# Decode scratch in PSUM, ELU with one VectorE pass, and a moved accumulator, in an LSH attention + Mish MoE + ELU MoE kernel on one core

## The chip, the cores and the metric

One core of a Trainium2 chip runs the whole program. The metric is the device time of one execution in microseconds (us), lower is better. Engines are named as in the profile: PE (TensorE matmul), PEld (its weight load), DVE (VectorE), ACT (ScalarE), POOL (GpSimd), SP (the engine that issues most transfers).

## The reference

Three layers follow each other; each one's output is the next one's x. Shapes: 2 batches, 8 heads, 768 tokens, head width 64; 1536 tokens in all, model width 512, inner width 2048.

```python
# 1. attention; a query sees the keys that hash into its bucket (6 sign bits)
mask   = q_bucket[:, :, :, None] == k_bucket[:, :, None, :]
scores = np.where(mask, scale * q @ k.T, -1e9)
x = softmax(scores) @ v                          # -> (1536, 512)
# 2. feed-forward with Mish
h = x @ w_in                                     # (1536, 2048)
x = (h * np.tanh(softplus(h))) @ w_out
# 3. feed-forward with ELU
h = x @ w_in2
y = np.where(h > 0, h, np.exp(np.minimum(h, 0)) - 1) @ w_out2
```

The weights arrive in HBM as 64-bit floats, and are turned into 32-bit parts on the chip.

## The kernel before

**Arithmetic.** TensorE multiplies in fp32r. To keep the precision each operand is split in a high and a low part, and a product is three matmuls: high*high, high*low, low*high (`products`, line 681). A 128x512 output needs 4 blocks of the inner dimension, so 12 matmuls. The split of an activation is an ACT cast (high) and a subtraction (low), `split`, line 753.

**Order.** No loop order is written down. Each operation is recorded with its engine, a cost, what it comes after and a priority, and a list scheduler (`Plan.run`, line 133) sets the order on every engine; buffers are rings (`Ring`), and an operation that needs a new buffer also waits for the last user of the oldest one. The planner's costs set the order alone; the chip then runs each engine's list in that order, each instruction waiting on semaphores. Attention with the first three weight units is planned first, the two feed-forward layers after it.

**Feed-forward.** The weights are 64 units of 128x512 numbers, 32 for each layer, half of them w_in and half w_out. An "up" step makes one accumulator h{unit}_{chunk} (a PSUM bank) from x and a unit, applies Mish or ELU and splits it into g{unit}_{chunk}; a "down" step sums four g into y_acc. There are three chunks of 512 tokens. Within the Mish layer, from unit 6 on, pairs of units do their chunks 0 and 2 in seven half products in place of eight (`pair_step`, line 758; banks b1 to b4, temporaries p and q from the ring gg_r); the sums of x that they need (T0, T1, T2) are made once by `turn` (line 833), which uses y_acc as scratch before y_acc is needed. `turn` runs 8 additions x_hi + x_lo, 8 subtractions, 8 ACT casts and 8 low parts; its additions and subtractions may go to DVE or POOL.

**Weight decode** (`convert`, line 271). A unit's raw 64-bit words (wraw) become a float by five DVE passes: L294 (shift and mask), L297 (and/or), L300 (compare and multiply), L302 (mask), L305 (low word times scale), one ACT Square (L292), then one ACT cast and two POOL passes make the high and low part w. Its scratch t, s (`wt`, `ws`) is in SBUF, two buffers of each.

**PSUM.** Eight banks. In the feed-forward layers six are the ring h_r, two the ring e_r: it holds the chunk-1 accumulators of the Mish layer, and in the ELU layer the exponentials.

**ELU** (`elu`, line 741). ACT makes exp(h) into e_ and tanh(h/2) into gg, DVE makes gg = (e_ + 1) * gg, which is exp(h) - 1, and then max(min(gg, 0), h).

**Reuse of SBUF.** When attention ends, the pool mp lies over attention's pool from the same address. A tile's first use waits for the last users of the attention tiles under it. y_acc is mp's first tile (24 KB per partition); the first tiles of attention's pool are ident, cst, sp (2.2 KB together; ident is the identity that every transpose reads, the last ones being those of rb, L590), then the heads' buffers.

Of the kernel before, what the change touches and what calls it, by code (L numbers as in the profile page):

```python
# [199 lines left out]
def kernel(ctx, tc, qk, v, w, tab, out):  # L200
# [70 lines left out]
    def convert(p, u, prio, keep=False):  # L271

        raw, ld = RAW.pop(u)
        t, s, w_ = Buf(wt_r, f"wt{u}"), Buf(ws_r, f"ws{u}"), Buf(wu_r, f"w{u}")

# [18 lines left out]
        o2 = p.op({DVE: dve(n, True)}, lambda e: nc.vector.tensor_scalar(  # L294
            out=ti(), in0=high(), scalar1=3, scalar2=0x3FFFFFF8, op0=ALU.logical_shift_left, op1=ALU.bitwise_and),
            [ld], [raw, t], prio, port=True)
        o3 = p.op({DVE: dve(n)}, lambda e: nc.vector.scalar_tensor_tensor(  # L297
            out=ti(), in0=high(), scalar=-0x40000000, in1=ti(), op0=ALU.bitwise_and, op1=ALU.bitwise_or),
            [o2], [raw, t], prio, port=True)
        o4 = p.op({DVE: dve(n)}, lambda e: nc.vector.scalar_tensor_tensor(  # L300
            out=t.tile, in0=s.tile, scalar=2.0 ** -30, in1=t.tile, op0=ALU.is_ge, op1=ALU.mult), [o1, o3], [s, t], prio, port=True)
        o5 = p.op({DVE: dve(n, True)}, lambda e: nc.vector.tensor_scalar(  # L302
            out=s.tile.bitcast(I32), in0=ti(), scalar1=-0x800000, scalar2=None, op0=ALU.bitwise_and),
            [o4], [s, t], prio, port=True)
# [19 lines left out]
    def sums(p, ue, uo, prio):  # L324
# [751 lines left out]
```

## Time and profile before

| | |
|---|---|
| median of 3 runs | 760.56 us (760.34 to 765.42) |
| profiled execution | 760.42 us, its span 758.6 us |
| PE busy | 744.9 us, 98% |
| DVE busy | 643.0 us, 85% |
| ACT, POOL busy | 431.0 us (57%), 363.1 us (48%) |
| chain that ended last | PE 78%, DVE 16%, ACT 2%, POOL 1% |

The span runs from the first to the last instruction; 1.8 us of the execution lie around it. PE's busy time alone doesn't tell what can be gained, since the ends of pipelined matmuls are modelled: the number of matmuls in a stretch and the distance from start to start do.

### The profile page before, as it was taken

The numbers are of one execution on the slowest core, as the hardware profiler recorded it, in microseconds if no ns is written. First come the engines' busy times: TensorE is split into PE (matmuls) and PEld (weight loads), VectorE is DVE, ScalarE is ACT, GpSimd is POOL, SyncE is SP. The second block draws the span as 40 slices with busy tenths as digits, with TensorE's granted clock in tenths as the row PEclk, the third lists the DMA queues.
The fourth block names the chain that finished last, engine by engine and source line by source line (L and its number), as shares of the span: only waits on it lengthen the run. The fifth ranks groups of instructions, "written<-read, shape, count | busy, mean of one in ns | idle before, by whom it ended". The sixth has DMA issues, their size and how long they took to land.

```text
span 758.6 us, 11117 instructions
## 1 busy us (share of the span) xinstructions
PE 744.9 (98%) x3936; PEld 645.8 (85%) x3936; DVE 643.0 (85%) x1118; ACT 431.0 (57%) x845; POOL 363.1 (48%) x274
## 2 busy tenths in 40 slices
PE   8999999999999799999999999999999999999998
PEld 7999999999988678888888888887888888888886
DVE  7899998999988989577696779999999999999442
ACT  5788888888885545543443346356556544443310
POOL 4345834743565655646536465863444423434100
PEclk9999999999999899999999999999999999999999
DMA  7776777686510121122111311112222212120012
GB/s 206 196 196 177 173 183 181 159 206 157 142 50 1 56 84 56 58 87 78 56 56 55 112 56 56 59 57 81 83 84 84 84 56 84 56 83 29 1 69 98
DMA packets 26983, 72.89 MB, mean 96 GB/s; under 512 B 6048, under 2 KB 7216, under 8 KB 26928
## 3 DMA queue, kind: packets, MB, share of 16 engines
q1 hardware_dynamic: 26784, 72.17, 32.3%
q8 instruction: 31, 0.51, 0.3%
q14 instruction: 24, 0.20, 0.1%
q10 hardware_dynamic: 144, 0.01, 0.0%
HBM read 45.76 MB, written 3.19 MB: 65 GB/s over the span
## 4 chain that ended last, share of the span: by engine, by line
PE 78%; DVE 16%; ACT 2%; issue 2%; POOL 1%; DMA 0%; DVEq 0%; POOLq 0%; ACTq 0%
PE h L688 47%; PE xt L575 8%; PE st L503 8%; PE tu L562 7%; PE h_b L688 7%; DVE ws L305 2%; DVE wt L297 2%; PE pj L425 2%; DVE wt L294 2%; DVE wt L300 2%; DVE ptl L258 1%; DVE g L258 1%; DVE pt L506 1%; DVE ws L302 1%; DVE gg L747 1%
## 5 line engine op out<-in xcount | busy, mean ns | idle before, releaser
L688 PE MATMUL h<-g,w 128*128 128x512 f32 x1140 | 267.0, 390 | 2.3 <-DVE g L258 1.6
L688 PEld LDWEIGHTS h<-g,w 128*128 128x128 f32 x1140 | 213.7, 188 | 48.5 <-DVE g L258 2.7
L688 PE MATMUL h<-x_hi,w 128*128 128x512 f32 x576 | 187.3, 394 | 3.9 <-DVE g L258 3.9
L258 POOL TENSOR_TENSOR wt<-wt,w 128x512 f32<-128x512 f32 x52 | 76.1, 1465 | 178.5 <-ACT w L253 84.9
L688 PEld LDWEIGHTS h<-x_hi,w 128*128 128x128 f32 x576 | 109.4, 190 | 27.1 <-DVE g L258 4.3
L688 PE MATMUL h<-x_lo,w 128*128 128x512 f32 x288 | 113.0, 392 | 0.0
L258 DVE TENSOR_TENSOR ptl<-tu,pth 128x512 fp32r<-128x512 f32 x144 | 96.1, 686 | 12.9 <-ACT pth L567 11.9
L511 ACT ACTIVATE pt<-pt,nb 128x768 f32<-128x768 f32 x96 | 90.4, 944 | 8.4 <-DVE nb L509 8.0
L567 ACT CAST pth<-tu 128x512 fp32r<-128x512 f32 x144 | 79.8, 587 | 26.4 <-PE tu L562 25.8
L506 DVE TENSOR_SCALAR_CACHE_REDUCE pt<-st 128x768 f32<-128x768 f32 x96 | 89.1, 950 | 1.4 <-PE st L503 0.9
L503 PE MATMUL st<-qkt 76*128 76x384 f32 (+1 forms) x384 | 81.5, 344 | 1.5 <-DVE qkt L432 0.8
L253 ACT CAST w<-wt 128x512 fp32r<-128x512 f32 x64 | 39.7, 623 | 73.0 <-DVE wt L300 50.6
L317 POOL TENSOR_TENSOR w<-wt,ws 128x512 fp32r<-128x512 f32 x52 | 72.5, 1394 | 17.5 <-DVE ws L305 12.8
L562 PE MATMUL tu<-ident,pt 128*128 128x128 f32 x576 | 80.0, 274 | 0.7 <-DVE ptl L258 0.6
L575 PE MATMUL xt<-pth,vt 128*128 128x256 f32 x288 | 79.1, 304 | 0.0
L983 DVE TENSOR_TENSOR y_acc<-h,y_acc 128x512 f32<-128x512 f32 x71 | 47.8, 686 | 32.5 <-PE h L688 32.4
L575 PE MATMUL xt<-ptl,vt 128*128 128x256 f32 x288 | 72.9, 282 | 0.0
L562 PEld LDWEIGHTS tu<-ident,pt 128*128 128x128 f32 x576 | 66.7, 140 | 5.9 <-DVE ptl L258 1.8
L503 PEld LDWEIGHTS st<-qkt 76*128 76x128 f32 (+1 forms) x384 | 64.1, 189 | 2.8 <-DVE pt L506 1.5
L253 ACT CAST g<-h 128x512 fp32r<-128x512 f32 x72 | 42.3, 587 | 40.6 <-DVE h L749 40.1
L305 DVE SCALAR_TENSOR_TENSOR ws<-wraw,ws 128x512 f32<-128x512 uint32 x64 | 64.0, 1000 | 0.9
L294 DVE TENSOR_SCALAR wt<-wraw 128x512 int32<-128x512 int32 x64 | 47.4, 746 | 20.3 <-POOL w L258 19.4
(106 smaller groups left out, 1149.1 us busy)
## 6 DMA issues: line engine op xcount, KB each, us to landing
wraw<-in_w_dram SPq DMA_DIRECT2D x64, 512.0 KB
qkt<-z SPq DMA_DIRECT2D x30, 384.0 KB
rw<-in_qk_dram SPq DMA_DIRECT2D x16, 384.0 KB
qkt<-z SPq DMA_DIRECT2D x31, 192.0 KB
vr<-in_v_dram SPq DMA_DIRECT2D x8, 384.0 KB
out_dram<-y_acc SPq DMA_DIRECT2D x11, 256.0 KB
rr<-dr SPq DMA_DIRECT2D x14, 192.0 KB
xs<-xr SPq DMA_DIRECT2D x14, 192.0 KB
```

Of the source, the lines that this page charges most:

```text
L253: nc.scalar.copy(out=out, in_=in_)
L258: eng(e).tensor_tensor(out=out, in0=a, in1=b, op=ALU.subtract)
L294: o2 = p.op({DVE: dve(n, True)}, lambda e: nc.vector.tensor_scalar(out=ti(), in0=high(), scalar1=3, scalar2=0x3FFFFFF8, op0=ALU.logical_sh ...
L305: o6 = p.op({DVE: dve(n)}, lambda e: nc.vector.scalar_tensor_tensor(out=s.tile, in0=low().bitcast(U32), scalar=2.0 ** -52, in1=s.tile, op0 ...
L317: o9 = p.op({POOL: pool(n)}, lambda e: nc.gpsimd.tensor_tensor(out=lo(), in0=t.tile, in1=s.tile, op=ALU.add), [o6, o8], [t, s, w_], prio)
L503: nc.tensor.matmul(st.tile[:, c, 0:HS], lhsT=wt.tile[0:n, q, t * 128:(t + 1) * 128], rhs=wt.tile[0:n, 2 + q, c * HS:(c + 1) * HS], start=( ...
L506: o = max_op = p.op({DVE: dve(S)}, lambda e: nc.vector.tensor_scalar(out=half(pt.tile), in0=st.tile[:, :, 0:HS], scalar1=-MASKED / SCALE, ...
L511: o = p.op({ACT: act(S, False) + 196}, lambda e: nc.scalar.activation(out=pt.tile, in_=pt.tile, func=AF.Exp, bias=nb.tile, scale=SCALE, ac ...
L562: nc.tensor.transpose(tu.tile[:, k, j], pt.tile[:, (2 * b + k) * 128:(2 * b + k + 1) * 128], ident)
L567: o = p.op({ACT: act(512)}, lambda e, tu=tu, ks=ks: nc.scalar.copy(out=hi.tile[:, ks], in_=flat(tu)), [o], [tu, hi], order(i, 'hi'))
L575: nc.tensor.matmul(xt.tile[:, 0:TH], lhsT=vt.tile[:, k, g % 2], rhs=m.tile[:, k], start=(k == 0 and j == 0), stop=(k == NKT - 1 and j == 1))
L688: nc.tensor.matmul(t.tile, lhsT=w_.tile[:, a, k], rhs=r, start=(start and n == 0), stop=(stop and n == 3 * len(ks) - 1), skip_group_check= ...
```

## The change

Four edits, taken together.

1. **Decode.** From unit 3 on (c_r is given), three scratch tiles a, b, d of a unit come from c_r, a ring over the two PSUM banks that were e_r: b is L294's result, a is Square's, d is L302's. The float t, the low part s and the parts w stay in SBUF. Every DVE pass of the decode then has a PSUM operand, and the planner no longer treats it as sharing a port with POOL; L294 is recorded ahead of Square.
2. **Accumulators.** Chunk-1 accumulators of the Mish layer go to h_r, which has the other six banks.
3. **ELU.** ACT makes Relu(-h) into gg, then exp(-gg) in place, DVE makes max(gg - 1, h): two ACT passes as before, one after the other, and one DVE pass in place of two.
4. **Layout.** gg_r has four buffers, and they are allocated first in mp (the "gap" tiles), so y_acc starts 8 KB further in, past ident, cst and sp. The scratch that the compiler reserves for dynamic DMA is 2 KB in place of 16, which makes room. The additions of `turn` go to POOL alone, and POOL passes are planned with other costs (pool2).

The core of the diff (renamed arguments of the other decode passes are left out; line numbers move by 6 to 12):

```diff
...
-    def convert(p, u, prio, keep=False):
+    def convert(p, u, prio, keep=False, c_r=None):
...
+        a, b, d = (Buf(c_r, f"c{u}_{i}") for i in range(3)) if c_r else (s, t, s)
+        port = not c_r
...
+        o2 = p.op({DVE: dve(n, port)}, lambda e: nc.vector.tensor_scalar(
+            out=bits(b), in0=high(), scalar1=3, scalar2=0x3FFFFFF8, op0=ALU.logical_shift_left, op1=ALU.bitwise_and),
+            [ld, *(HELD if c_r else ())], [raw, t, b], prio, port=port)
         o1 = p.op({ACT: act(n, False)}, lambda e: nc.scalar.activation(
-            out=s.tile, in_=high().bitcast(F32), func=AF.Square), [ld, *HELD], [raw, s], prio)
...
+            out=a.tile, in_=high().bitcast(F32), func=AF.Square), [ld, *HELD, o2 if c_r else None], [raw, s, a], prio)
...
-            out=s.tile, in0=low().bitcast(U32), scalar=2.0 ** -52, in1=s.tile, op0=ALU.mult, op1=ALU.mult),
-            [o5], [raw, s], prio, port=True)
+            out=s.tile, in0=low().bitcast(U32), scalar=2.0 ** -52, in1=d.tile, op0=ALU.mult, op1=ALU.mult),
+            [o5], [raw, s, d], prio, port=port)
+        cost = pool2(n) if c_r else pool(n)
...
-        y_acc = mp.tile([128, NX, NT], F32, name="y_acc")
...
-        gg_r = ring(3, [128, TC], F32, "gg")
+        gg_r = ring(NGG, [128, TC], F32, "gg")
+        [mp.tile([128, TC], F32, tag="gg", name=f"gap{i}", bufs=NGG) for i in range(NGG)]
+        y_acc = mp.tile([128, NX, NT], F32, name="y_acc")
...
-        e_r = Ring(2, lambda n: banks[1].tile([128, TC], F32, tag="e", name=n, bufs=2))
+        c_r = Ring(2, lambda n: banks[1].tile([128, TC], F32, tag="e", name=n, bufs=2))
...
             a = p.op({ACT: act(n)}, lambda e: nc.scalar.activation(
-                out=e_.tile, in_=t.tile, func=AF.Exp), [x, table[0]], [t, e_], prio)
-            b = p.op({ACT: act(n)}, lambda e: nc.scalar.activation(
-                out=gg.tile, in_=t.tile, func=AF.Tanh, scale=0.5), [x, table[0]], [t, gg], prio)
+                out=gg.tile, in_=t.tile, func=AF.Relu, scale=-1.0), [x, table[0]], [t, gg], prio, lat=60)
+            a = p.op({ACT: act(n, False)}, lambda e: nc.scalar.activation(
+                out=gg.tile, in_=gg.tile, func=AF.Exp, scale=-1.0), [a, table[0]], [gg], prio)
             a = p.op({DVE: dve(n)}, lambda e: nc.vector.scalar_tensor_tensor(
-                out=gg.tile, in0=e_.tile, scalar=1.0, in1=gg.tile, op0=ALU.add, op1=ALU.mult), [a, b], [e_, gg], prio)
-            a = p.op({DVE: dve(n)}, lambda e: nc.vector.scalar_tensor_tensor(
-                out=t.tile, in0=gg.tile, scalar=0.0, in1=t.tile, op0=ALU.min, op1=ALU.max), [a], [t, gg], prio)
+                out=t.tile, in0=gg.tile, scalar=1.0, in1=t.tile, op0=ALU.subtract, op1=ALU.max), [a], [t, gg], prio)
...
-                    t = Buf(e_r if kind == 0 and c == 1 else h_r, f"h{u}_{c}")
+                    t = Buf(h_r, f"h{u}_{c}")
...
```

**What moves on the engines.** PE's list is the same up to the first pair of units, and holds the same matmuls to the end. DVE's list is the same to the end of attention, and is then another one. Its first twelve entries after the last low part of x, before (g is an activation's low part, wt, ws decode scratch, wraw a raw unit; the number behind a name's last underscore only tells buffers apart):

```order
L294 TENSOR_SCALAR wt3_3692<-wraw3_3159 128x512
L294 TENSOR_SCALAR wt4_3696<-wraw4_3351 128x512
L297 SCALAR_TENSOR_TENSOR wt3_3692<-wraw3_3159,wt3_3692 128x512
L258 TENSOR_TENSOR g0_0_3694<-h0_0_3465,g0_0_3694 128x512
L258 TENSOR_TENSOR g1_0_3714<-h1_0_3605,g1_0_3714 128x512
L300 SCALAR_TENSOR_TENSOR wt3_3692<-ws3_3690,wt3_3692 128x512
L297 SCALAR_TENSOR_TENSOR wt4_3696<-wraw4_3351,wt4_3696 128x512
L302 TENSOR_SCALAR ws3_3690<-wt3_3692 128x512
L300 SCALAR_TENSOR_TENSOR wt4_3696<-ws4_3710,wt4_3696 128x512
L305 SCALAR_TENSOR_TENSOR ws3_3690<-wraw3_3159,ws3_3690 128x512
L302 TENSOR_SCALAR ws4_3710<-wt4_3696 128x512
L258 TENSOR_TENSOR g2_0_3730<-h2_0_3612,g2_0_3730 128x512
```

And the same place of the changed kernel, on DVE too (c is the scratch in PSUM):

```order
L303 TENSOR_SCALAR c3_1_3695<-wraw3_3159 128x512
L303 TENSOR_SCALAR c4_1_3701<-wraw4_3351 128x512
L264 TENSOR_TENSOR g0_0_3698<-h0_0_3465,g0_0_3698 128x512
L308 SCALAR_TENSOR_TENSOR wt3_3694<-wraw3_3159,c3_1_3695 128x512
L308 SCALAR_TENSOR_TENSOR wt4_3700<-wraw4_3351,c4_1_3701 128x512
L264 TENSOR_TENSOR g1_0_3718<-h1_0_3605,g1_0_3718 128x512
L311 SCALAR_TENSOR_TENSOR wt3_3694<-c3_0_3725,wt3_3694 128x512
L311 SCALAR_TENSOR_TENSOR wt4_3700<-c4_0_3739,wt4_3700 128x512
L313 TENSOR_SCALAR c3_2_3747<-wt3_3694 128x512
L313 TENSOR_SCALAR c4_2_3754<-wt4_3700 128x512
L316 SCALAR_TENSOR_TENSOR ws3_3724<-wraw3_3159,c3_2_3747 128x512
L316 SCALAR_TENSOR_TENSOR ws4_3738<-wraw4_3351,c4_2_3754 128x512
```

The decode of units 3 and 4 now runs side by side, and g0_0 stands one place earlier. Further on in DVE's list of before, the entries that lead up to g3_0, the low part that the down step of unit 4 waits for:

```order
L258 TENSOR_TENSOR g2_1_3856<-h2_1_3797,g2_1_3856 128x512
L258 TENSOR_TENSOR g2_2_3863<-h2_2_3816,g2_2_3863 128x512
L302 TENSOR_SCALAR ws5_3827<-wt5_3829 128x512
L258 TENSOR_TENSOR T1_1_3678<-y_acc_3674,T1_1_3678 128x512
L305 SCALAR_TENSOR_TENSOR ws5_3827<-wraw5_3760,ws5_3827 128x512
L258 TENSOR_TENSOR T2_1_3680<-y_acc_3674,T2_1_3680 128x512
L294 TENSOR_SCALAR wt6_3904<-wraw6_3784 128x512
L258 TENSOR_TENSOR g3_0_3902<-h3_0_3844,g3_0_3902 128x512
```

The same place on DVE in the changed kernel:

```order
L264 TENSOR_TENSOR g2_1_3873<-h2_1_3809,g2_1_3873 128x512
L316 SCALAR_TENSOR_TENSOR ws5_3847<-wraw5_3774,c5_2_3875 128x512
L264 TENSOR_TENSOR g2_2_3882<-h2_2_3833,g2_2_3882 128x512
L264 TENSOR_TENSOR T1_1_3682<-y_acc_3678,T1_1_3682 128x512
L264 TENSOR_TENSOR T2_1_3684<-y_acc_3678,T2_1_3684 128x512
L311 SCALAR_TENSOR_TENSOR wt6_3827<-c6_0_3900,wt6_3827 128x512
L313 TENSOR_SCALAR c6_2_3923<-wt6_3827 128x512
L316 SCALAR_TENSOR_TENSOR ws6_3899<-wraw6_3781,c6_2_3923 128x512
L264 TENSOR_TENSOR g3_0_3925<-h3_0_3861,g3_0_3925 128x512
```

The whole decode of unit 6 now stands ahead of g3_0, where one pass of it stood before. From the last low part of x up to g3_0 DVE has 36 entries before and 37 now. On POOL the passes of `turn` still stand right behind the last entry of attention.

## Rows read from the trace of the kernel before

**Rows 1.** The page: busy time of each engine (share of the span) and instructions.

```profile
PE 744.9 (98%) x3936; PEld 645.8 (85%) x3936; DVE 643.0 (85%) x1118; ACT 431.0 (57%) x845; POOL 363.1 (48%) x274
```

**Rows 2.** Windows: stretch, length, busy PE, PEld, DVE, ACT, POOL; granted clock; DMA.

```profile
235.00:262.00 27.00, 23.13 (x92) 18.63 (x91) 25.69 (x28) 14.36 (x26) 21.06 (x14) 0.87 0.12 40
...
300.00:500.00 200.00, 200.00 (x881) 165.03 (x880) 157.40 (x227) 88.96 (x158) 116.88 (x92) 1.00 0.19 66
500.00:540.00 40.00, 38.70 (x170) 31.50 (x169) 39.28 (x63) 25.84 (x49) 15.84 (x12) 1.00 0.19 66
```

**Rows 3.** PE's longest waits after 240: line, releaser, us in total, times, longest.

```profile
PE h L688 <- DVE g L258: 5.4, 4, 3.9
```

**Rows 4.** Timeline of PE, 247 to 261: start, us, operation, count [idle before].

```profile
248.52 0.39 PE L688 MATMUL h<-x_hi,w 128*128 128x512 f32 x1
252.78 0.79 PE L688 MATMUL h<-x_hi,w 128*128 128x512 f32 x1 [3.87 <-DVE g L258]
...
258.66 0.62 PE L688 MATMUL h<-x_hi,w 128*128 128x512 f32 x2
```

**Rows 5.** Timeline of DVE, 235 to 253.

```profile
236.93 2.94 DVE L294 TENSOR_SCALAR wt<-wraw 128x512 int32<-128x512 int32 x2
...
248.12 1.76 DVE L305 SCALAR_TENSOR_TENSOR ws<-wraw,ws 128x512 f32<-128x512 uint32 x1
...
251.21 1.51 DVE L258 TENSOR_TENSOR g<-h,g 128x512 fp32r<-128x512 f32 x2
```

**Rows 6.** Timeline of POOL, 235 to 252.5.

```profile
235.43 5.60 POOL L838 TENSOR_TENSOR y_acc<-x_hi,x_lo 128x512 f32<-128x512 f32 x4 [8.49 <-PE r L590]
...
250.97 2.68 POOL L258 TENSOR_TENSOR wt<-wt,w 128x512 f32<-128x512 f32 x2
```

**Rows 7.** Lines of DVE: tiles, shapes, count | busy us, mean ns | idle before.

```profile
L305 DVE SCALAR_TENSOR_TENSOR ws<-wraw,ws 128x512 f32<-128x512 uint32 x64 | 64.0, 1000 | 0.9
L297 DVE SCALAR_TENSOR_TENSOR wt<-wraw,wt 128x512 int32<-128x512 int32 x64 | 58.9, 924 | 0.7
L300 DVE SCALAR_TENSOR_TENSOR wt<-ws,wt 128x512 f32<-128x512 f32 x64 | 52.4, 820 | 1.7
...
L294 DVE TENSOR_SCALAR wt<-wraw 128x512 int32<-128x512 int32 x64 | 47.4, 746 | 20.3 <-POOL w L258 19.4 <-POOL w L317 0.9
...
L302 DVE TENSOR_SCALAR ws<-wt 128x512 int32<-128x512 int32 x64 | 37.8, 591 | 1.0
L749 DVE SCALAR_TENSOR_TENSOR h<-gg,h 128x512 f32<-128x512 f32 x48 | 32.7, 690 | 0.6
```

**Rows 8.** Timeline of PE, 270.9 to 278.6 and 528 to 532.

```profile
271.78 5.73 PE L688 MATMUL h<-g,w 128*128 128x512 f32 x24 [0.26 <-DVE g L258]
278.13 0.74 PE L688 MATMUL h<-g,w 128*128 128x512 f32 x2 [0.61 <-DVE g L258]
...
527.65 1.75 PE L688 MATMUL h<-g,w 128*128 128x512 f32 x7
530.01 0.49 PE L688 MATMUL h<-g,w 128*128 128x512 f32 x1 [0.61 <-ACT g L253]
531.19 1.20 PE L688 MATMUL h<-g,w 128*128 128x512 f32 x4 [0.68 <-DVE g L258]
```

**Rows 9.** Timeline of DVE, 252 to 275.

```profile
260.67 0.41 DVE L294 TENSOR_SCALAR wt<-wraw 128x512 int32<-128x512 int32 x1
261.00 0.68 DVE L838 TENSOR_TENSOR y_acc<-y_acc 128x512 f32<-128x512 f32 x1
261.60 0.68 DVE L297 SCALAR_TENSOR_TENSOR wt<-wraw,wt 128x512 int32<-128x512 int32 x1
...
271.05 1.27 DVE L258 TENSOR_TENSOR g<-h,g 128x512 fp32r<-128x512 f32 x2
```

**Rows 10.** Timeline of ACT, 249 to 252.

```profile
250.41 0.58 ACT L737 ACTIVATE h<-h 128x512 f32<-128x512 f32 x1
250.93 0.60 ACT L253 CAST w<-wt 128x512 fp32r<-128x512 f32 x1
```

More of the change, by code (lines that the diff above doesn't have):

```diff
@@ L70, in pool, with pool2 @@
     return 150 + 2.1 * n
+def pool2(n):
+    return 150 + 2.38 * n
 class Buf:
@@ L294, in convert @@
[L294 to L296 removed]
+            out=a.tile, in_=high().bitcast(F32), func=AF.Square), [ld, *HELD, o2 if c_r else None], [raw, s, a], prio)
         o3 = p.op({DVE: dve(n)}, lambda e: nc.vector.scalar_tensor_tensor(
[L298 to L299 removed]
+            out=ti(), in0=high(), scalar=-0x40000000, in1=bits(b), op0=ALU.bitwise_and, op1=ALU.bitwise_or),
@@ L300, in convert @@
+            [o2], [raw, t, b], prio, port=port)
         o4 = p.op({DVE: dve(n)}, lambda e: nc.vector.scalar_tensor_tensor(
[L301 to L304, printed above, removed]
+            out=t.tile, in0=a.tile, scalar=2.0 ** -30, in1=t.tile, op0=ALU.is_ge, op1=ALU.mult), [o1, o3], [a, t], prio, port=port)
@@ L305, in convert @@
+        o5 = p.op({DVE: dve(n, port)}, lambda e: nc.vector.tensor_scalar(
+            out=bits(d), in0=ti(), scalar1=-0x800000, scalar2=None, op0=ALU.bitwise_and),
+            [o4], [d, t], prio, port=port)
         o6 = p.op({DVE: dve(n)}, lambda e: nc.vector.scalar_tensor_tensor(
-            out=s.tile, in0=low().bitcast(U32), scalar=2.0 ** -52, in1=s.tile, op0=ALU.mult, op1=ALU.mult),
-            [o5], [raw, s], prio, port=True)
+            out=s.tile, in0=low().bitcast(U32), scalar=2.0 ** -52, in1=d.tile, op0=ALU.mult, op1=ALU.mult),
+            [o5], [raw, s, d], prio, port=port)
@@ L308, in convert @@
+        cost = pool2(n) if c_r else pool(n)
         if keep:
-            o7 = p.op({POOL: pool(n)}, lambda e: nc.gpsimd.tensor_tensor(
+            o7 = p.op({POOL: cost}, lambda e: nc.gpsimd.tensor_tensor(
                 out=t.tile, in0=t.tile, in1=s.tile, op=ALU.add), [o6], [t, s], prio)
             o8 = p.op({ACT: act(n, False)}, lambda e: copy(e, hi(), t.tile), [o7], [t, w_], prio)
-            o9 = p.op({POOL: pool(n)}, lambda e: sub(e, lo(), t.tile, f32(hi())), [o8], [t, w_], prio)
+            o9 = p.op({POOL: cost}, lambda e: sub(e, lo(), t.tile, f32(hi())), [o8], [t, w_], prio)
@@ L315, in convert @@
             o7 = p.op({ACT: act(n, False)}, lambda e: copy(e, hi(), t.tile), [o4], [t, w_], prio)
-            o8 = p.op({POOL: pool(n)}, lambda e: sub(e, t.tile, t.tile, f32(hi())), [o5, o7], [t, w_], prio)
-            o9 = p.op({POOL: pool(n)}, lambda e: nc.gpsimd.tensor_tensor(
+            o8 = p.op({POOL: cost}, lambda e: sub(e, t.tile, t.tile, f32(hi())), [o5, o7], [t, w_], prio)
+            o9 = p.op({POOL: cost}, lambda e: nc.gpsimd.tensor_tensor(
                 out=lo(), in0=t.tile, in1=s.tile, op=ALU.add), [o6, o8], [t, s, w_], prio)
@@ L329, in sums @@
         wa, wb = Buf(wu_r, f"wa{ue}"), Buf(wu_r, f"wb{ue}")
-        cost = {POOL: pool(256)}
+        cost = {POOL: pool2(256)}
         def tt(out, x, y, op, after, uses):
@@ L833, in turn @@
         def turn(prio):
-            either = {DVE: dve(n), POOL: pool(n)}
+            either = {DVE: dve(n), POOL: pool2(n)}
             def tt(out, a, b, op, after):
-                return p.op(either, lambda e: eng(e).tensor_tensor(out=out, in0=a, in1=b, op=op), after, (), prio, port=True)
+                return p.op({POOL: pool2(n)} if op == ALU.add else either, lambda e: eng(e).tensor_tensor(out=out, in0=a, in1=b, op=op), after, (), prio, port=True)
             done = []
@@ L934, in moe @@
                     fetch(p, u, first[u] - LEADF)
-                convert(p, u, first[u] - LEADC, u in pairs or u - 1 in pairs)
+                convert(p, u, first[u] - LEADC, u in pairs or u - 1 in pairs, c_r)
             if u - 1 in pairs:
```

12 lines of the change are left out of this document (8 added, 4 removed).

## The prediction

> **What bounds the kernel now.** I read the page first, then windows by stretch, then PE's waits, and then the engines' timelines around each wait. PE is busy 98% of the span [rows 1], so what can be won is the time in which it doesn't start a matmul when it could. In the quiet stretch 300 to 500 it starts 881 matmuls in 200.00 us [rows 2], 0.227 us each: that is the floor, since the change adds and takes away no matmul. After 240 us PE waits for DVE four times, 5.4 us in all [rows 3]. Three places hold nearly all of it.
>
> *The start of the Mish layer.* One matmul starts at 248.52, the next at 252.78, and the fifteenth behind the first at 258.66 [rows 4]. Fifteen take 3.41 us at 0.227, and they took 10.14: 6.73 lost. 4.03 of it is the wait (4.26 less 0.23); the other 2.70 is the clock, whose mean in this stretch is 0.87 [rows 2]: the matmuls after the wait ran at the lower of the two levels. PE wanted h2_1's accumulator, which in a ring of two banks is h0_1's, and that is free when DVE has made g0_1: DVE's two g end at 252.72 [rows 5]. DVE was late because of the decode. Two passes of L294 took 1.47 us each and one of L305 1.76 [rows 5]; the same L294 takes 0.41 alone and the two-operand passes 0.68, with the next entry 0.60 after the start [rows 9]. The eleven entries from 236.93 to 251.21 took 1.30 each. Beside them POOL ran the sums of x without a gap, 1.40 each, having sat idle 8.49 us until attention's last transposes [rows 6].
>
> *The first down steps.* 24 matmuls from 271.78 end at 277.23, the next starts at 278.13: 0.91 lost, for g3_2. Its neighbour g3_0, which DVE makes at 271.05, cost an idle 0.26 just before [rows 8, 9].
>
> *The first ELU units.* 530.01 to 531.19 is 1.18 for one matmul, 0.95 lost, and the seven from 527.65 were through at 529.24, 0.77 ahead of 530.01: 1.72 in both [rows 8]. DVE is busy 39.28 of 40 us there [rows 2].
>
> **The change, part by part.** The sum is made on the profiled execution, 760.42 us, 0.14 under the median of the runs.
>
> *Decode.* Its five passes now average 0.75, 0.92, 0.82, 0.59 and 1.00, 4.08 us a unit [rows 7]. No pass of before has its new form. The nearest row for the three two-operand ones is L749, one operand in PSUM and one in SBUF: 0.69 on average over 48 [rows 7], in stretches where POOL was busy about 40% (15.84 of 40 us [rows 2]). For L294 and L302, one operand in and one out with one of them in PSUM, the bounds are 0.41 (alone, SBUF to SBUF) and 0.69; I take a slot of 0.60, the distance of two starts [rows 9]. So 3.3 to 3.5 us a unit, 0.6 to 0.8 saved, 37 to 49 us of DVE over 61 units. Almost all of that lies beside a PE that is full, and is worth nothing. It counts at the three places.
>
> A rule speaks against this edit. The Trainium skill, VectorE: DVE Perf Modes, "Why PSUM operands drop a tier", says that an fp32 instruction with a PSUM operand loses the two-results-a-cycle mode. By it L294 and L302 would go from 0.41 to about 0.69 where they ran alone; with the slot of 0.60 the sum stays as it is. No run here shows the new form yet.
>
> *First wait.* y_acc no longer lies on the identity of the last transposes, so POOL can begin where its idle time began, 235.43 - 8.49 = 226.94 [rows 6], and has nine passes of 1.3 to 1.4 behind it by 239. DVE's fourteen entries up to g0_1, at 0.60 from 237.5 where ACT can feed it (ACT's starts are 0.52 apart [rows 10]), reach g0_1 at 245.9 and g0_2 at 246.5 and end it at 247.2 (an estimate from these rows). With six banks h2_1 takes h1_0's, free behind the sixth entry, about 241.6; PE asks at 248.75. h3_0 takes h0_1's, free at 246.6, and unit 3, whose four POOL passes (1.34 each [rows 6]) begin at 243.2 and end at 248.6; PE asks 24 matmuls later, at 254.2. Both hold: **-6.73**.
>
> *What is late next.* PE wants g3_0 69 matmuls after 248.75, at 264.4. DVE has 22 entries behind g0_2, from 247.2 on, g3_0 the last: 13.2 us at 0.60. The planner has put the whole decode of unit 6 ahead of it. Seven of them (T1_0, T2_0, T0_1, T1_1, T2_1 and two subtractions of y_acc) still have both operands in SBUF, and each that meets a running POOL pass may take 1.76 in place of 0.68 [rows 5, 9], 1.08 more. Four such meetings, 4.3, are my count, since POOL has a queue of its own at the first three and the last ones; and some 1.5 is DVE's wait for ACT, whose casts stand behind the same subtractions. 247.2 + 13.2 + 4.3 + 1.5 + 0.1 is 266.3: a new wait of about **+2.0** where 0.26 goes (**-0.26**). Bounds: no meeting gives no wait, seven give 5.2. I take the four, in the middle, because POOL was gapless here before [rows 6]. g3_2 comes seven entries behind g3_1, with unit 7's decode between, and 0.91 stays.
>
> *ELU.* 48 passes of 0.69 leave DVE, 33 us [rows 7]; ACT has two passes as before, the second behind the first, about 0.1 later, which 0.69 less on DVE covers. In 500 to 540 twelve chunks save 8 us and four units 3, off 39.28: DVE is no limit there, and **-1.72** goes.
>
> *Attention's end.* POOL's sums now run beside the last low parts of x, DVE passes on SBUF alone. One stands ahead of a low part that PE needs at once; it may be held by up to one POOL pass of 1.4 and PE has some work in hand: **+0.3**, between 0 and 1.
>
> *At nothing:* the reserved scratch and the fourth gg buffer; transfers leave from SP and are the same; if gg had to wait it would cost ACT alone, which is idle 43% [rows 1].
>
> Sum: 760.42 - 6.73 - 0.26 - 1.72 + 2.0 + 0.3 = **754.0**.
>
> **The rivals.**
>
> *All waits go* (chance 0.27). For it: without meetings g3_0 is ready at 262.0, and g3_2 follows earlier. 754.0 - 2.0 - 0.91 - 0.3 = 750.8.
>
> *The new wait also lowers the clock* (0.13). For it: the wait of 3.87 did [rows 4]. Against: waits of 0.6 left it at 1.00 in 500 to 540 [rows 2, 8], and 2.0 lies between. A like price of 2.70: 756.7.
>
> *Slower: accumulators run short* (0.06). Six banks serve all of Mish, not eight. In each of its six pair blocks a later accumulator now takes the bank of b3 27 matmuls, 6.1 us, after b3's last. Its release needs a DVE addition, Mish, a cast and a subtraction, 0.69 + 0.58 + 0.60 + 0.69 [rows 7, 10], 2.6 us, so it decides where over 3.5 us of queue stand ahead. At the start of Mish DVE was 10 us behind: g0_1 ended at 252.72 [rows 5] for an accumulator whose last matmul stands 27 ahead of 248.75, so at 242.6. Were that so at all six, 4 us and a clock drop of 2.7 each: 754.0 + 40 = 794; at half of them 774. Against: 300 to 500 has no wait, and DVE gets lighter.
>
> The Trainium skill, Perfetto Trace Analysis, "Matmul Optimizations", says that all 8 PSUM banks should serve matmuls; the change gives it up for two. The rows of before can't show what that costs.
>
> *The decode doesn't get lighter* (0.06): passes with one PSUM operand still meet POOL. Then DVE's lateness stays, softened by POOL's earlier start, and the first wait keeps half: about 758.
>
> **Numbers.** My forecast 0.48, with the four rivals 1. Likeliest: 754.0 us. Its own range, from two to six meetings, is 752 to 756.2. For eight in ten I take 749.5 to 758: it holds the case with no wait and the one with the clock, and leaves out the slow one and the two tails. A difference of 1% is about what a measurement can tell, 752.95 here: faster has the 0.27 and 0.15 of my own, 0.42; slower than 768 has 0.06; the same 0.52.
>
> **What would show it.** PE's timeline at 248.75 without a gap, and the clock at 1.00 throughout; DVE's L303 to L316 at 0.6 to 0.7 beside a busy POOL; POOL's first sum at 227; a PE wait for a g between 264 and 268; none at 520. I'd be wrong if a wait came back in every pair block, if T passes ran at 0.68, or if DVE's decode passes were above 0.8.

## The result, and the profile after

The changed kernel takes 751.87 us (median of ten executions, 751.0 to 758.05; the kernel before 760.59 on the same chip). The measured ratio is 0.9875 with a 95% interval of 0.9844 to 0.9906 (the two medians alone give 0.9885). So it is faster by 0.9 to 1.6%; whether by more than the 1% that the prediction took as its bound isn't settled. The forecast was 754.0, with 749.5 to 758.0 for eight times in ten. The profiled execution took 751.72 us, its span 749.9.

"Lost" means below the distance from one matmul's start to the next less the pace of 0.227 us. PE's order and number of matmuls hardly change, so what is lost behind attention can be added up gap by gap: about 10.8 us before, 1.8 us after.

The page's busy line, and the windows that answer to [rows 2]: stretch, length, then busy time of PE, PEld, DVE, ACT and POOL with instruction counts, granted clock, DMA share, GB/s.

```profile
PE 741.5 (99%) x3936; PEld 645.0 (86%) x3936; DVE 578.7 (77%) x1067; ACT 432.0 (58%) x845; POOL 343.8 (46%) x277
...
235.00:262.00 27.00, 27.00 (x121) 22.31 (x120) 23.99 (x36) 18.34 (x35) 19.44 (x15) 1.00 0.12 41
262.00:285.00 23.00, 21.73 (x95) 17.32 (x95) 17.43 (x27) 13.53 (x26) 15.41 (x14) 1.00 0.28 96
500.00:540.00 40.00, 40.00 (x179) 33.10 (x178) 31.86 (x51) 26.13 (x48) 14.25 (x11) 1.00 0.23 79
```

The wait at 248.5 is gone: PE is busy all of 235 to 262, and the clock there is 1.00 where it was 0.87. In 500 to 540 PE is busy all 40 us and DVE 31.86, down from 39.28. DVE as a whole fell by 64.3 us [rows 1], while the execution got 8.7 shorter. What is left stands in the second window, and PE's waits behind 235 and its timeline name it (start, length, what ended the idle time before):

```profile
PE h L700 <- DVE g L264: 1.3, 2, 1.1
```

```profile
265.22 0.39 PE L700 MATMUL h<-g,w 128*128 128x512 f32 x1
266.71 5.73 PE L700 MATMUL h<-g,w 128*128 128x512 f32 x24 [1.10 <-DVE g L264]
272.61 3.70 PE L700 MATMUL h<-g,w 128*128 128x512 f32 x15 [0.17 <-DVE g L264]
```

From 265.22 to 266.71 are 1.49 us, 1.26 lost, for g3_0; at 272.05 another 0.34 is lost for g3_2; each is followed by one more distance that is 0.11 too long. DVE's timeline shows why g3_0 is late, and POOL's and DVE's rows at attention's end show the other loss:

```profile
246.26 2.02 DVE L264 TENSOR_TENSOR g<-h,g 128x512 fp32r<-128x512 f32 x3
248.20 2.57 DVE L264 TENSOR_TENSOR T<-y_acc,T 128x512 fp32r<-128x512 f32 x2
250.69 1.78 DVE L849 TENSOR_TENSOR y_acc<-y_acc 128x512 f32<-128x512 f32 x1
...
261.61 2.38 DVE L264 TENSOR_TENSOR T<-y_acc,T 128x512 fp32r<-128x512 f32 x2
263.92 0.68 DVE L311 SCALAR_TENSOR_TENSOR wt<-c,wt 128x512 f32<-128x512 f32 x1
264.63 0.69 DVE L313 TENSOR_SCALAR c<-wt 128x512 int32<-128x512 int32 x1
265.36 0.69 DVE L316 SCALAR_TENSOR_TENSOR ws<-wraw,c 128x512 f32<-128x512 uint32 x1
265.97 1.28 DVE L264 TENSOR_TENSOR g<-h,g 128x512 fp32r<-128x512 f32 x2
```

```profile
227.12 5.01 POOL L849 TENSOR_TENSOR y_acc<-x_hi,x_lo 128x512 f32<-128x512 f32 x4
```

```profile
231.18 1.23 DVE L264 TENSOR_TENSOR x_lo<-xr,x_hi 128x256 fp32r<-128x256 f32 x1
```

The same low part in the kernel before:

```profile
230.99 0.42 DVE L258 TENSOR_TENSOR x_lo<-xr,x_hi 128x256 fp32r<-128x256 f32 x1
```

g0_1 and g0_2 end the row of 246.26 and are through at 248.28; before, g0_1 alone ended at 252.72, as the second in the row of 251.21 [rows 5]. The turn's T and y_acc passes have both operands in SBUF and still meet POOL: 1.78 for one that takes 0.68 alone. Behind them come three decode passes of unit 6, and only then g3_0. At attention's end a low part of x that took 0.42 before now takes 1.23, since POOL's sums begin at 227.12; the first matmul of h0_1 comes 18.45 us behind the first of h0_0, and came 17.83 behind it before.

The decode's passes, over all units (count, busy us, mean ns, then idle time before):

```profile
L313 DVE TENSOR_SCALAR c<-wt 128x512 int32<-128x512 int32 x61 | 42.1, 692 | 1.5
L311 DVE SCALAR_TENSOR_TENSOR wt<-c,wt 128x512 f32<-128x512 f32 x61 | 41.9, 689 | 7.5 <-ACT c L306 4.0
L316 DVE SCALAR_TENSOR_TENSOR ws<-wraw,c 128x512 f32<-128x512 uint32 x61 | 41.6, 684 | 1.4
L308 DVE SCALAR_TENSOR_TENSOR wt<-wraw,c 128x512 int32<-128x512 int32 x61 | 41.6, 683 | 10.9 <-POOL w L264 7.8
L303 DVE TENSOR_SCALAR c<-wraw 128x512 int32<-128x512 int32 x61 | 41.6, 684 | 2.3 <-DMA wraw<-in_w_dram 2.3
...
L313 DVE TENSOR_SCALAR ws<-wt 128x512 int32<-128x512 int32 x3 | 1.2, 417 | 0.0
```

All five are at 0.68 to 0.69, 3.43 us a unit where they were 4.08 [rows 7], whether POOL runs or not: of these 305 passes none took over 0.70, where before single passes of the same lines took up to 1.79. The last row is the same L313 for the three units that are still decoded in SBUF, during attention: 417 ns.

### The profile page after: what moved, and what is told of

Same layout as the page of the kernel before. It is cut to its first block, busy times and chain, and to the rows that moved or that the text cites. A ratio compares the mean times of both kernels' runs of the same rounds, so it can differ in the third digit from the quotient of the medians.

```text
span 749.9 us, 11074 instructions
## 1 busy us (share of the span) xinstructions
PE 741.5 (99%) x3936; PEld 645.0 (86%) x3936; DVE 578.7 (77%) x1067; ACT 432.0 (58%) x845; POOL 343.8 (46%) x277
## 4 chain that ended last, share of the span: by engine, by line
PE 88%; DVE 7%; ACT 3%; DMA 1%; issue 1%; SPq 0%; POOL 0%; ACTq 0%; DVEq 0%; POOLq 0%
PE h L700 56%; PE h_b L700 8%; PE st L515 7%; PE xt L587 7%; PE tu L574 7%; PE pj L437 2%; DVE ptl L264 2%; DVE pt L518 1%; DMA qkt<-z 1%; DMA wraw<-in_w_dram 1%; ACT pt L523 1%; DVE g L264 0%; PE warm L669 0%; DVE x_lo L264 0%; ACT g L259 0%
## 5 line engine op out<-in xcount | busy, mean ns | idle before, releaser
L700 PE MATMUL h<-x_hi,w 128*128 128x512 f32 x576 | 184.6, 390 | 0.0
L264 POOL TENSOR_TENSOR wt<-wt,w 128x512 f32<-128x512 f32 x52 | 67.4, 1297 | 196.4 <-ACT w L259 105.0
L264 DVE TENSOR_TENSOR g<-h,g 128x512 fp32r<-128x512 f32 x72 | 49.2, 688 | 30.2 <-ACT g L259 29.2
L329 POOL TENSOR_TENSOR w<-wt,ws 128x512 fp32r<-128x512 f32 x52 | 68.0, 1309 | 7.7 <-DVE ws L316 4.2
L700 PEld LDWEIGHTS h<-x_lo,w 128*128 128x128 f32 x288 | 54.1, 188 | 10.9
L760 DVE SCALAR_TENSOR_TENSOR h<-gg,h 128x512 f32<-128x512 f32 x48 | 33.1, 691 | 35.6 <-ACT gg L758 35.6
```

Source lines behind the costliest of these rows:

```text
L264: eng(e).tensor_tensor(out=out, in0=a, in1=b, op=ALU.subtract)
L329: o9 = p.op({POOL: cost}, lambda e: nc.gpsimd.tensor_tensor(out=lo(), in0=t.tile, in1=s.tile, op=ALU.add), [o6, o8], [t, s, w_], prio)
L700: nc.tensor.matmul(t.tile, lhsT=w_.tile[:, a, k], rhs=r, start=(start and n == 0), stop=(stop and n == 3 * len(ks) - 1), skip_group_check= ...
L760: a = p.op({DVE: dve(n)}, lambda e: nc.vector.scalar_tensor_tensor(out=t.tile, in0=gg.tile, scalar=1.0, in1=t.tile, op0=ALU.subtract, op1= ...
```

## The experiments

Two theories stood against each other for the first wait, which is three quarters of the gain. L: the place of y_acc made it, since it kept POOL's sums back until 235.4. D: the decode in SBUF made it, since its passes meet POOL whenever POOL runs. For ELU: E, the second DVE pass made the waits at 530, or D, the decode did. Each ratio is to the kernel before, timed in the same round on the same chip. The rounds ran on different chips, and the median of the kernel before was 760.59 to 761.62 in them, so a difference of a microsecond between medians of two runs says little by itself; the lost time in their traces says more.

### The placement alone

The kernel before, with y_acc behind the gap tiles; NGG is 4, and the reserved scratch is 2 KB as in the change. No engine's order changes.

```diff
...
-        y_acc = mp.tile([128, NX, NT], F32, name="y_acc")
...
-        gg_r = ring(3, [128, TC], F32, "gg")
+        gg_r = ring(NGG, [128, TC], F32, "gg")
+        [mp.tile([128, TC], F32, tag="gg", name=f"gap{i}", bufs=NGG) for i in range(NGG)]
+        y_acc = mp.tile([128, NX, NT], F32, name="y_acc")
...
```

> The kernel before with the change's placement of y_acc alone (four gap tiles ahead of it, a fourth gg buffer, 2 KB of reserved scratch); the order of every engine is that of before. Theory L (the place of y_acc made the first wait): POOL's first sum at 227 in place of 235.4, no gap in PE at 248.5, clock 1.00 there; the 0.95 and 0.77 at 530 stay; 760.5 - 6.7 + 0.6 at attention's end = 754.4 us. Theory D (the weight decode on SBUF is what held DVE, whenever POOL runs beside it): POOL's conversion passes now meet the same decode passes, g0_1 comes only partly earlier, a gap of 1 to 3 us and the clock's 2.7 stay; 757 to 760 us.

Measured: 754.99 us, ratio 0.9915 (0.9885 to 0.9945). One window and PE's timeline of this kernel:

```profile
235.00:262.00 27.00, 27.00 (x121) 22.30 (x121) 26.27 (x37) 18.69 (x35) 15.60 (x12) 1.00 0.11 40
```

```profile
524.64 0.50 PE L689 MATMUL h<-g,w 128*128 128x512 f32 x1 [0.59 <-ACT g L254]
525.82 0.98 PE L689 MATMUL h<-g,w 128*128 128x512 f32 x3 [0.67 <-DVE g L259]
```

L held: the whole first wait and its clock go without any change to the decode. Its passes still meet POOL (the two shifts at 237.96 take 2.95 us), but POOL is done with its first sums at 240.6 and then idle for 4 us, and DVE ends g0_1 and g0_2 in time. The waits at 524 stay, as expected, and so do those for g3_0 and g3_2 (0.87 and 0.88 lost).

### The changed kernel with the old placement

Every engine's order is that of the changed kernel; y_acc is the first tile of mp again, and the gap tiles are left out (gg keeps its four buffers).

> The changed kernel with y_acc back in its old place, over attention's identity; the order of every engine is that of the changed kernel. Theory L: POOL's sums start at 235.4 again and the first wait comes back, 4 us and the clock's 2.7, less the 0.6 at attention's end: 751.9 + 6.1 = 758 us. Theory D: the decode's passes with an operand in PSUM stay at 0.68 to 0.70 beside POOL's sums, g0_1 is through by 248, and no gap comes at 248.5; the turn's subtractions are late by some 2 us, so the wait for g3_0 grows by 1 to 2: 752 to 753.5 us.

Measured: 758.79 us, ratio 0.9956 (0.9928 to 0.9984). L's time, but not L's mechanism. A window, PE's timeline and ACT's:

```profile
262.00:285.00 23.00, 17.27 (x67) 13.57 (x66) 18.82 (x28) 14.27 (x27) 15.91 (x14) 0.85 0.19 69
```

```profile
267.96 0.50 PE L700 MATMUL h<-g,w 128*128 128x512 f32 x1 [2.75 <-ACT g L259]
271.44 2.92 PE L700 MATMUL h<-g,w 128*128 128x512 f32 x6 [2.98 <-DVE g L264]
```

```profile
242.03 0.62 ACT L259 CAST T<-y_acc 128x512 fp32r<-128x512 f32 x1 [3.83 <-POOL y_acc L848]
242.56 0.58 ACT L259 CAST g<-h 128x512 fp32r<-128x512 f32 x1
```

Nothing is lost at 248.5, as D had it, and the decode's passes run at 0.68 beside POOL; but D's time of 752 to 753.5 is missed by 5 us. ACT's cast of T0_0, which needs POOL's sums, stands ahead of g0_0's cast, so all that follows on ACT and DVE is 4 us late. The wait comes 16 to 20 us later, at g3_0, twice 3 us long, and takes the clock down to 0.85 there. So in this order the light decode without POOL's earlier start moves the wait and doesn't remove it.

### The same, with three casts moved on ACT

T0_0's cast goes behind unit 4's Square, those of T1_0 and T2_0 behind g0_2's cast. The planner's finished list is reordered for it, with nothing else changed on any engine. In `moves` each operation of a list goes behind the one named first, and what depends on it follows; DEC holds a unit's Square and five passes, CAST the casts of the turn:

```diff
...
+                    p.moves += [(DEC[4][0], [CAST[1, 0]]), (CAST["g"], [CAST[2, 0], CAST[4, 0]])]
```

> The changed kernel with y_acc in its old place, as in the run of that kind that took 758.8 us, and three entries of ACT's queue moved: the casts T0_0, T1_0 and T2_0 of the turn, each of which waits for POOL's sums, behind the casts of the first units. Theory Q (in that run T0_0's cast stood at the head of ACT's queue from 238.2 to 242.0 and made all behind it late): g0_0 comes at 239 in place of 243, the waits of 2.9 and 3.3 us at 265 to 271 shrink to 1.5 to 2.5 in all, the clock stays at 1.00 there: 752 to 753 us. Rival P (POOL's lateness itself, through the turn's passes in DVE's queue): T2_0 still waits for POOL until 250 and meets its passes, most of the wait stays: 756 to 759 us.

> A second look at the kernel with y_acc in its old place and the turn's casts moved on ACT: in the first look one DVE pass (T1_0) took 9.83 us while POOL ran eight passes without a gap. Theory V (whether DVE gets its turn between two POOL passes differs from execution to execution): T1_0 takes under 2 us here, POOL's passes beside it 1.7, and the time is 754.5 us, as most of its runs were. Rival: the hold is that of the instruction order and comes each time: about 9.8 us again, 759.6 us.

Measured: 755.15 us, ratio 0.9926 (0.9904 to 0.9949); a second run of the same kernel, one execution, 759.35. Both profiled executions took over 759 us while six of the eight timed ones took 754.5 to 755.8, so the trace isn't that of the usual execution. The median lies between Q's 752 to 753 and P's 756 to 759. g0_0 came at 239.2 as Q said, and g0_1 and g0_2 were through at 247.2. What followed was on neither theory's list (second run, DVE and then POOL):

```profile
245.19 1.88 DVE L276 TENSOR_TENSOR g<-h,g 128x512 fp32r<-128x512 f32 x3
247.95 10.43 DVE L276 TENSOR_TENSOR T<-y_acc,T 128x512 fp32r<-128x512 f32 x2 [0.88 <-ACT T L271]
```

```profile
247.21 1.31 POOL L276 TENSOR_TENSOR T<-y_acc,T 128x512 fp32r<-128x512 f32 x1
248.46 1.31 POOL L863 TENSOR_TENSOR y_acc<-y_acc 128x512 f32<-128x512 f32 x1
249.71 2.55 POOL L276 TENSOR_TENSOR wt<-wt,w 128x512 f32<-128x512 f32 x2
252.20 2.54 POOL L341 TENSOR_TENSOR w<-wt,ws 128x512 fp32r<-128x512 f32 x2
254.69 2.54 POOL L863 TENSOR_TENSOR y_acc<-x_hi,x_lo 128x512 f32<-128x512 f32 x2
```

DVE's T1_0 began at 247.95 and took 9.83 us of these 10.43: it waited while POOL ran eight passes without a gap, each at its free 1.31, and ended 0.55 behind the last of them, at 257.78. The first run shows the same 9.83. In both, PE then loses 2.1 us at 260, and behind that 2.9 and 3.3 us in the first and 1.3 and 3.3 in the second; the clock of 262 to 285 is 0.85 in both. In the changed kernel the two engines took turns instead (DVE 1.78, POOL 1.74). The Trainium skill, SBUF — State Buffer, "Who interferes with whom", says that the SBUF port pair that the two engines share is an exclusive lock, and that a DVE instruction with two SBUF inputs contends for it with a GpSimd instruction that reads SBUF. The passes of 1.78, against 0.68 alone, agree with a lock held for one POOL pass; the 9.83, through eight of them, is more than that section tells. The rival to theory V held for the second run: the same hold and 759.35. As both traces are of executions over 759, they don't tell whether the shorter ones had the hold too, so V isn't refuted; what decides whether DVE gets its turn stays open.

### ELU

The changed kernel with the old ELU (its first scratch from gg_r), and the kernel before with the new ELU alone. The diff is that of the first; the second has the ELU of the change:

```diff
...
-                out=gg.tile, in_=t.tile, func=AF.Relu, scale=-1.0)
-                out=gg.tile, in_=gg.tile, func=AF.Exp, scale=-1.0)
-                out=t.tile, in0=gg.tile, scalar=1.0, in1=t.tile, op0=ALU.subtract, op1=ALU.max)
+                out=e_.tile, in_=t.tile, func=AF.Exp)
+                out=gg.tile, in_=t.tile, func=AF.Tanh, scale=0.5)
+                out=gg.tile, in0=e_.tile, scalar=1.0, in1=gg.tile, op0=ALU.add, op1=ALU.mult)
+                out=t.tile, in0=gg.tile, scalar=0.0, in1=t.tile, op0=ALU.min, op1=ALU.max)
```

> The changed kernel with the old ELU (Exp, Tanh and two VectorE passes, its first scratch taken from the gg ring in SBUF). PE's order is that of the changed kernel. Theory E (the second VectorE pass made the waits at 530): DVE busy over 39 of 40 us in 500 to 540, the 1.7 us of waits there come back, 753.6 us. Theory D (the decode's 0.6 to 0.8 a unit is enough): 36 to 37.5 of 40 us, waits there under 0.4 in all, 751.9 to 752.3 us.

> The kernel before with the new ELU alone (Relu, Exp, one VectorE pass); decode and layout as before. Theory E (the second VectorE pass made the waits at 530): DVE's 39.3 us of 500 to 540 fall to about 36, the 1.8 us of waits and lost matmul time there go, the first wait and its clock stay: 760.5 - 1.8 = 758.7 us. Rival: DVE is late there because of the decode, which is untouched, and half or more of the waits stay: 759.6 to 760.5 us.

Measured: 753.97 us for the first (ratio 0.9892, 0.9854 to 0.9929), 759.78 for the second (0.9984, 0.9966 to 1.0002). The same window of each, in that order:

```profile
500.00:540.00 40.00, 39.84 (x176) 32.67 (x175) 38.48 (x62) 26.38 (x50) 13.44 (x11) 1.00 0.19 70
```

```profile
500.00:540.00 40.00, 39.49 (x175) 32.37 (x174) 37.66 (x57) 29.45 (x53) 21.04 (x14) 1.00 0.25 79
```

Before, 1.83 us were lost around 530 (0.77, 0.95 and 0.11). With the light decode and the old ELU 0.44 is left there, and another 0.44 stands at 591; with the old decode and the new ELU 0.78 is left. So either edit takes more than half of what the ELU layer loses, and it needs both to take all: neither E nor D held as stated. The second kernel's interval reaches across 1, so its gain shows in the lost time and not clear of noise in the time. The first kernel's median is 2.1 us above the changed kernel's, more than its added 0.8 us of lost time: in its profiled execution the layers' first matmul came at 223.0 in place of 220.3, in attention, which the edit doesn't touch.

### Placement and ELU, without the decode in PSUM

The kernel before with both edits; in the Mish layer all eight banks serve accumulators.

> The kernel before with the placement of y_acc and the new ELU, so the changed kernel less the decode in PSUM, with all eight banks for accumulators. Theory N (the decode in PSUM saves DVE time that nothing waits for): the lost matmul time after 236, 4.8 us in the run with the placement alone, loses the 2.3 us at 524, and 2 to 2.6 us of short waits for g3_0, g3_2 and at 290 stay: 752.3 to 753 us, within 1 us of the changed kernel. Theory D (the decode in PSUM is needed once ELU is light): waits of 3 us as in the run with the decode in SBUF and six banks, with the clock's 2.7: 755 us or more.

Measured: 753.63 us, ratio 0.9915 (0.9900 to 0.9930). PE's waits behind 236:

```profile
PE h L689 <- DVE g L259: 1.7, 3, 0.6
```

Theory N nearly held: no wait over 0.6 us and no drop of the clock. Against the changed kernel 3.4 us are lost behind 236 and not 1.8: the waits at 524, at 290 and in two pair blocks. The medians lie 1.76 apart, above N's 1 us, but the intervals of the two ratios overlap. So the decode in PSUM is worth some 1.6 us here, together with the planner's other costs, the additions on POOL alone and the order that come with it; no run parts these.

### The changed kernel with the decode in SBUF

Accumulators keep six banks, the two others stay empty. The planner's costs for the decode change too, and with them the order: DVE's and ACT's lists differ from the changed kernel's from the start of Mish on, PE's from the first pair block on.

```diff
...
-                convert(p, u, first[u] - LEADC, u in pairs or u - 1 in pairs, c_r)
+                convert(p, u, first[u] - LEADC, u in pairs or u - 1 in pairs)
```

> The changed kernel with the decode's scratch in SBUF again for all units of the layers; the two PSUM banks stay unused, so accumulators have six banks as in the changed kernel. Theory D: decode passes average 0.8 to 1.0 in 237 to 270 where POOL runs beside them, some wait at the start of Mish is back, 754 to 758 us. Theory L: POOL is done with its sums by 239, the decode passes run at 0.4 to 0.7, no gap at 248.5, 751 to 752.5 us. If accumulators run short once DVE is late (the rival that ends slower), waits come in the six pair blocks of 300 to 500: over 760 us.

> A second look at the changed kernel with the decode's scratch in SBUF: its first look took 760 us, with a wait of 2.9 us for g6_1's accumulator at 309 and the lower clock behind it, while most of its runs were near 755. Theory B (six banks leave the pair block no slack once DVE is late, and how late it is differs): the wait at 309 is under 0.5 us or gone, the clock stays at 1.00, 754 to 755 us, with short waits for g3_0 left. Rival: the wait at 309 is there in each execution and the time differs elsewhere.

Measured: 755.97 us, ratio 0.9937 (0.9908 to 0.9965); a second run of the same kernel 755.64. PE, ACT and POOL in the second:

```profile
309.12 2.44 PE L700 MATMUL h<-g,w 128*128 128x512 f32 x6 [2.79 <-DVE g L264]
```

```profile
306.72 0.62 ACT L259 CAST wa<-sa 128x512 fp32r<-128x512 f32 x1 [0.44 <-POOL sa L345]
307.24 0.61 ACT L259 CAST w<-wt 128x512 fp32r<-128x512 f32 x1
307.76 0.58 ACT L259 CAST g<-h 128x512 fp32r<-128x512 f32 x1
```

```profile
303.21 1.28 POOL L321 TENSOR_TENSOR wt<-wt,ws 128x512 f32<-128x512 f32 x1 [2.68 <-DVE ws L316]
```

No wait at 248.5, as L had it, but one of 2.79 in the first pair block, in both runs (the clock of 300 to 330 falls to 0.94 in the second and 0.89 in the first). It is the rival "accumulators run short" at one place: h9_1 wants the bank of h6_1, which has gone through Mish at 305.6. The cast that frees it then stands behind a copy and two casts of the next pair's weights on ACT (wa10, w11), until 307.76. Of these 2.2 us, 0.44 is a wait for POOL, which had itself waited 2.68 us for DVE's last decode pass of unit 11.

That the slower passes made this wait is not shown, since the order is another one. In the changed kernel the cast of g6_1 is no earlier, behind three casts of weights (ACT there):

```profile
306.72 0.58 ACT L750 ACTIVATE h<-h 128x512 f32<-128x512 f32 x1 [3.65 <-PE h L700]
...
308.77 0.58 ACT L259 CAST g<-h 128x512 fp32r<-128x512 f32 x1
```

Still the first matmul of h9_1 starts there at 307.20 with nothing lost. PE takes up h6_1 at 301.76 in that order, behind h8's accumulators and h9_0, so that h9_1 falls on the bank of h8_0. Here it takes up h6_1 at 288.49, ahead of h8_0, and h9_1 falls on h6_1's; the planner's own plan already leaves PE idle at that place. Theory D thus got its time, 754 to 758, by a wait that isn't the one at the start of Mish. Theory B fell: the wait is there each time, and the two runs differ by the start of the layers (3.1 us) and the clock.

### The two waits that are left

First g3_0 and g3_2 alone are moved on DVE, ahead of passes of units 6 and 7 and of the turned x; then also, on ACT, w6's cast and three entries behind it are moved behind g3_2's cast. The diff is that of the second run; the first has only the move of g3_0 and, for g3_2, of the two low parts and unit 7's last pass (SPH[-1] is g3_2's cast; KEEP[6] is the cast and low part of w6, TD[3, j] are the low parts of the turned x).

```diff
...
+                if (kind, f, c) == (0, 3, 0):
+                    p.moves.append((G[f, c][1], DEC[6][3:]))
+                if (kind, f, c) == (0, 3, 2):
+                    p.moves += [(SPH[-1], [*KEEP[6], DEC[7][0], CAST[3, 0], CAST[3, 1]]),
+                                (G[f, c][1], [TD[3, 0], TD[3, 1], *DEC[7][1:]])]
```

> The changed kernel with two entries of DVE's queue moved and nothing else: g3_0 ahead of unit 6's last three decode passes, g3_2 ahead of unit 7's last pass and two low parts of the turn. Theory T (the two waits left are DVE's queue order): g3_0 starts at 263.9 and g3_2 before 270.9, both gaps go, 1.49 + 0.56 less 2 x 0.23, and 0.22 behind them: 751.9 - 1.8 = 750.1 us. Rival: three decode passes 0.6 later make unit 6's weights late for its first product at 280: a wait of up to 0.6 there, 750.7 us; or the low parts moved meet POOL's passes and the wait comes back for the turned x, 751.5 us.

> The changed kernel with g3_0 and g3_2 moved ahead on DVE as before, and on ACT the cast of w6, two casts of the turned x and unit 7's Square moved behind the Mish and the cast of g3_2. Theory A (in the last run of this kind g3_2 was late because ACT stood at w6's cast, which waits for POOL until 267.85, with h3_2's Mish behind it): Mish of h3_2 starts by 265.5, g3_2 is through by 267.7, the gap at 270 to 272 (0.76, 0.50 and 0.11 us over the pace) goes, 751.2 - 1.4 = 749.8 us. Rival: unit 7's decode and the turned x, now later by 1.3 us, are late for the products at 282 to 286, and a wait of 0.5 to 1.5 comes there: 750.5 to 751.3 us.

Measured: 751.20 us for the first (0.9882, 0.9866 to 0.9897), 749.78 for the second (0.9859, 0.9843 to 0.9875). PE's and ACT's timeline of the first:

```profile
265.01 5.60 PE L714 MATMUL h<-g,w 128*128 128x512 f32 x24
271.21 0.49 PE L714 MATMUL h<-g,w 128*128 128x512 f32 x1 [0.60 <-ACT g L271]
```

```profile
267.85 0.62 ACT L271 CAST w<-wt 128x512 fp32r<-128x512 f32 x1 [3.81 <-POOL wt L333]
268.38 0.62 ACT L318 ACTIVATE c<-wraw 128x512 f32<-128x512 f32 x1
268.94 1.13 ACT L271 CAST x_hi<-y_acc 128x512 fp32r<-128x512 f32 x2
269.96 0.58 ACT L764 ACTIVATE h<-h 128x512 f32<-128x512 f32 x1
```

g3_0's wait is gone, but most of it came back at g3_2: ACT stood 3.81 us at w6's cast, with unit 7's Square, two casts and then the Mish of h3_2 behind it. Half of theory T failed there: 1.4 us are lost at g3_2 in place of the 1.8 at both. With the ACT entries moved as well (a window and PE's timeline of the second):

```profile
262.00:285.00 23.00, 23.00 (x103) 19.03 (x103) 17.39 (x26) 13.00 (x25) 15.00 (x14) 1.00 0.25 82
```

```profile
265.24 10.13 PE L715 MATMUL h<-g,w 128*128 128x512 f32 x44
```

PE has no idle time left behind 236, and theory A's 749.8 us was met. Nothing came back at the products of 282 to 286, where its rival had a wait. This version has a lower median than the changed kernel by 2.1 us, near the 1.8 us of lost time that its trace no longer has. The intervals of the two ratios overlap.

## Why the prediction was right, and where it was off

The forecast time and its range held, and the sign of the result was given 0.42 against 0.52 for "the same". By the prediction's own terms, in us of the profiled executions:

| step | predicted | measured |
|---|---|---|
| first wait and its clock | -6.73 | -6.73, nothing lost from 236 to 265 |
| ELU at 530 | -1.72 | -1.83 |
| g3_0: new wait less the old | +1.74 | +0.84 (1.37 lost, 0.53 before) |
| g3_2 | 0 | -0.43 (0.45 lost, 0.88 before) |
| attention's end | +0.3 | +0.62 |
| short waits at 295 and in pair blocks | not in the sum | -0.86 |
| sum | -6.4 | -8.4, and -8.7 in all |

The 0.3 between the two last numbers lies at the ends: the layers start 0.2 later, the program ends 0.35 sooner behind its last matmul, and the rest is rounding. Most terms erred to the same side; the time lies inside the range for eight in ten, and just below the forecast's own range of 752 to 756.2.

- **First wait.** The walk of POOL and DVE was good to 1.1 us: POOL's first sum at 227.12 (227 predicted), g0_2 through at 248.28 (247.2). Its mechanism was only half stated. It credits POOL's earlier start and the slot of 0.60 together, and the runs part them: the placement alone gives all of it, the light decode without it moves it to g3_0.
- **The new wait.** Right in place and cause. DVE had g3_0 ready for PE at 266.7, 266.3 predicted; three meetings took 1.78 each and one 0.87 (T1_0, the first in the row of 248.20), where four of 1.76 were counted. The mis-sized term is when PE asks: not at 264.4 but at 265.45, of which 0.8 is the later start of the layers and attention's end, so 1.26 are lost and not 2.0. The likeliest case thus ended between the forecast and the rival "all waits go" (750.8), which the last run reached with 749.8.
- **"g3_2 ... 0.91 stays"** failed. PE, held 1.26 at g3_0, comes later to g3_2, which DVE made from 271.88, and loses 0.34 there where it lost 0.77: a wait ahead of another takes part of it away. When g3_0's wait was taken out, 1.37 were lost at g3_2.
- **Short waits** were not in the sum, which was made of "three places" that "hold nearly all of it"; 0.42 at 295 and 0.22 in each of two pair blocks add up to 0.86. So "300 to 500 has no wait" wasn't quite true.
- **ELU.** The size was right. DVE's busy time in 500 to 540 fell by 7.4 us, where 11 were counted; it was enough.
- **Attention's end.** The mechanism, a low part of x held by a POOL pass, was exact (1.23 us for 0.42). It cost 0.62 and not 0.3, inside the stated 0 to 1; PE had less work in hand than supposed.
- **Decode.** 3.3 to 3.5 us a unit predicted, 3.43 measured. The rule of the Trainium skill, VectorE: DVE Perf Modes, "Why PSUM operands drop a tier", agrees with the trace: L313 takes 692 ns with one operand in PSUM and 417 with both in SBUF (on int32, where the section speaks of fp32). It decided nothing, since the slower pass was never held by POOL.
- **The rivals.** A wait of 1.26 didn't lower the clock (1.00 in 262 to 285). Accumulators didn't run short in the changed kernel; the mechanism is real, though, and cost 3 us and the clock in the run with the decode in SBUF, whose order puts h9_1 on h6_1's bank. The run with eight banks for accumulators and without the decode in PSUM was not faster (753.63 against 751.87), but no run changes the number of banks alone.

## What to carry to other kernels

A wait is best removed where the lateness begins. Here that was POOL's start: moving one buffer took the whole first wait, with DVE's passes and ACT's casts as they were. The cheaper passes without that start moved the wait to another accumulator, since ACT's casts handed the same 4 us on. Before a pass is made cheaper, look whether the work beside it can start earlier, for a buffer's address may hold it back. Once the large waits are gone, the next ones are entries of in-order queues that wait for another engine with urgent work behind them, and moving a few of them took away as much lost time here (1.8 us) as the lighter decode did (1.6).

## What the runs showed of the hardware

- A DVE pass with both operands in SBUF can wait through more than one POOL pass: 9.83 us behind eight passes without a gap, twice, where elsewhere the two engines took turns (1.78 and 1.74).
- With the decode's scratch in PSUM POOL got faster too: in the run with the old placement its passes took 1.29 to 1.30 beside the decode's from 243.8 to 249.3, and 1.46 to 1.74 in that stretch before.
- Waits of 1.26 us, and of 0.76 and 0.50 close together, left the granted clock at 1.00. After one of 2.8 starts were 0.427 apart, the lower of the two levels, and the mean of the 30 us around it was 0.94 and 0.89 in two executions; after two of 2.75 and 2.98 close together the mean of 262 to 285 was 0.85. Right behind a wait of 2.0 starts were 0.427 apart in one of the two executions of the run with three casts moved, and not in the other, so the prediction's rival, by which its new wait of 2.0 also lowers the clock, is not refuted by the 1.26 that came.
